# One transpose, three masks and four products moved between the first two units of a cached-attention block

## The chip, the cores and the metric

The kernel runs on one core of one Trainium2 chip. Its time is device microseconds of one execution; the median of three runs is compared. A profile of one further execution shows what each engine did and when: PE (matrix products), DVE (vector), ACT (scalar, also called ScalarE), POOL, and SP, the queue from which nearly all transfers are issued. The transfers themselves are carried out by the core's 16 DMA engines.

## The reference

One decode step of a transformer block with conditioning, for two batch rows of width 512. What matters here is the attention over a sliding block of the cache:

```
mod = silu(c) @ w_mod                      # six shifts, scales and gates
h = layernorm(x) * (1 + ca) + sa
q = h @ wq                                 # 32 query heads of 128, one position
k, v = last 4096 rows of the caches        # 8 key/value heads, each for 4 query heads
o = softmax(q k^T / sqrt(128)) v
x = x + ga * (o @ wo)
x = x + gb * (silu((layernorm(x) * (1 + cb) + sb) @ w1) @ w2)
```

All numbers are float32. 2 batch rows x 8 heads x 4096 rows x 128 numbers make 33.6 MB of keys and as much of values; with the weights the kernel reads 97.5 MB.

## The kernel before

All big tiles lie in `store`, three slots of 64 KB a partition, 8.39 MB each. A slot holds one load: first `w_mod` and `wq`, later one unit's keys or values, at the end the weights `wo`, `w1`, `w2`. The attention is cut into four units t = 0 to 3; a unit is one batch row and four key/value heads (`seq[t]`). Its keys `kt[t]` are one load of 8.39 MB, its values `vt[t]` another.

The loads of keys (k) and values (v) come in the order k0, k1, v0, k2, v1, k3, v2, v3 and take the slots 0, 1, 2 in turn. `fetch(n)` issues them up to the n-th. A load waits on SP until the last reader of its slot is done, and all later loads wait behind it, for SP runs its instructions in the order of the program. So k2 goes into slot 0 once the last product that reads unit 0's part of it is done, v1 into slot 1 after unit 1, and k3 into slot 2 after unit 0's values have been used.

The program is recorded operation by operation (class `Flow`; every operation therefore carries line 117 in the profile) and emitted in this order, with semaphore waits where an operation needs another engine's result or overwrites what another engine still reads. Each engine runs its own operations strictly in the order in which they were written down. For one unit they are:

- `scores(t)`: eight times DVE transposes an eighth of the keys in place (`STREAM_TRANSPOSE`, 128x2048) and PE multiplies it with the queries `qbd` (a group of four products; the profile shows two records for each). The eight groups fill the two halves f = 0, 1 of `bankA`, four each.
- the softmax, still inside `scores(t)`: maximum on DVE (`mx`), two small products on PE that spread it, `bias` and the exponentials on ACT, written into the first 1024 columns of the unit's key slot.
- `turn(t)`: DVE transposes these 1024 columns; four masks (`zp`, 128x512 each, a multiplication with a column of `key`) spread them over four copies, three on DVE and one on ACT; then four products with `gather` on PE collect them into `bankC`. They are the last readers of the slot.
- `spread(t)`: four ACT copies from `bankC` to `ptb`, the left operand of the products with the values.
- `values(t - 1, ...)`: the products of the unit before with its values, in two parts around `turn(t)`, and `collect(t - 1)`, which adds them up.

Unit 0 has no unit before it, so its `turn` and `spread` follow its softmax directly, and then `fetch(4)` issues k2.

Of the kernel before, what the change touches and what calls it, by code (L numbers as in the profile page):

```python
# [12 lines left out]
G = HQ // HKV  # L13
U = 4
# [121 lines left out]
def adaln_block(nc, x, k_cache, v_cache, wq, wo, w1, w2, c, w_mod, out):  # L136
# [7 lines left out]
    pe, dve, act, pool, sp = fl.pe, fl.dve, fl.act, fl.pool, fl.sp  # L144
# [4 lines left out]
    NK = W // 32  # L149
# [6 lines left out]
    bank_a = nc.alloc_psum_tensor("bankA", [P, 1024], F32).ap()  # L156
# [6 lines left out]
    def bank(tag):  # L163
        banks[tag].append(banks[tag].pop(0))
        return banks[tag][-1]
# [25 lines left out]
    def const(shape, name):  # L191
        return buf(name, *shape)
# [17 lines left out]
    kt, vt = {}, {}  # L210

    def load_cache(cache, t, where):
        hh, b = seq[t]
        sp.dma_start(
            where,
            cache[b, U * hh : U * hh + U, SK - W :, :].rearrange(
                "u (i n) d -> i u (n d)", n=NK
            ),
        )
        return where  # L220
# [59 lines left out]
    qbd = const([P, 2, 4, B, 4, 16], "qbd")  # L280
# [54 lines left out]
    for s0, s1, m in ((0, 2, m_a), (2, 6, m_b)):  # L335
        for k in range(4):
            v = wm[:, k].rearrange("p (s g m) -> p g s m", s=6, g=4)
            for g in range(4):
# [4 lines left out]
                    start=(k == 0),  # L343
                    stop=(k == 3),
# [22 lines left out]
    for n in range(2):  # L367
        for k in range(4):
            wv = wqt[:, k].rearrange("p (n s g m) -> p n g s m", n=2, s=4, g=G)
            for g in range(G):  # L370
# [4 lines left out]
                    start=(k == 0),  # L375
                    stop=(k == 3),
                )
    for n in range(2):
        qT = early(4, 4, 32)
        dve.transpose(qT.rearrange("p s j r -> p (s j r)"), q_ps[n])  # L380
        for g in range(G):
            r = slice(32 * g, 32 * g + 32)
# [8 lines left out]
        for i in range(4):  # L391
            r = slice(32 * i, 32 * i + 32)
# [7 lines left out]
    mx, bias = const([P, 1], "mx"), const([P, 1], "bias")  # L400
    o_all = bank("O")[:, : B * DH].rearrange("p (b d) -> p b d", b=B)

    def scores(t):
        hh, b = seq[t]
        kv = kt[t].rearrange("p (n j r) -> p n j r", n=NK, j=4)
        for f in range(2):
            for j in range(4):

                kT = kv[:, 64 * f : 64 * f + 64, j, :]
                dve.transpose(kT, kT)  # L410
                for u in range(U):
                    pe.matmul(
                        bank_a[32 * u : 32 * u + 16, 512 * f : 512 * f + 512],
                        qbd[:, hh, u, b, j, :],
                        kT[:, :, u:32:U],
                        start=(j == 0),
                        stop=(j == 3),
                    )
        mrow = kt[t][0:1, 3072:3200]
        pool.memset(mrow, 0.0)  # L420
        dve.tensor_reduce(mx, bank_a, axis=AX.X, op=ALU.max)
        mT = bank("B")
        pe.matmul(mT[0:1, :P], mx, sel, start=True, stop=True)
        dve.tensor_reduce(
            mg,
            mT[0:1, :64].rearrange("o (a g u) -> o g u a", g=G, u=U),
            axis=AX.X,
            op=ALU.max,
        )
        dve.tensor_copy(  # L430
            mrow.rearrange("o (u v a g) -> o u v a g", u=U, v=2, g=G)[:, :, 0],
            mg.rearrange("o g u -> o u g")[:, :, None, :].to_broadcast([1, U, 4, G]),
        )
        bp = bank("B")
        pe.matmul(bp[:, 0:1], mrow, negscale, start=True, stop=True)
        act.copy(bias, bp[:, 0:1])
        act.activation(
            kt[t][:, :1024], bank_a, AF.Exp, bias=bias, scale=SCALE, accum_out=rowsum[:, t : t + 1]
        )

    tp = bank("C")

    def turn(t):
        pr = kt[t][:, :1024]
        dve.transpose(pr, pr)
        xp = pr.rearrange("p (f k w) -> p f k w", f=2, w=32)
        zp = kt[t][:, 1024:3072].rearrange("p (n f k w) -> p n f k w", n=4, f=2, w=16)
        for n in range(4):
            if n < 3:
                dve.tensor_scalar(zp[:, n], xp[:, :, :, :16], key[:, n : n + 1], None, op0=ALU.mult)  # L450
            else:
                act.activation(zp[:, n], xp[:, :, :, :16], AF.Copy, scale=key[:, n : n + 1])
        for a in range(4):
            pe.matmul(
                tp[32 * a : 32 * a + 32],
                gather,
                zp.rearrange("p n f k w -> p (f k) n w")[:, :, :, G * a : G * a + G],
                start=True,
                stop=True,
            )  # L460

    def spread(t):
        for u in range(U):
            act.activation(
                ptb[:, :, G * u : G * u + G], tp.rearrange("p (n g) -> p n g", g=G), AF.Copy,
                scale=par[:, u : u + 1],
            )
# [3 lines left out]
    def values(t, n0, n1, n):  # L471

        for n0 in range(n0, n1, n):
            if n0 == 0:
                o_ps[t] = bank("D")
            c = n0 // n % (8 // n)
            r, d0 = 16 * n * c, n0 % 4 * DH
            pe.matmul(
                o_ps[t][r : r + 16 * n, d0 : d0 + n * DH],
                ptb[:, n0 : n0 + n, :].rearrange("p n w -> p (n w)"),  # L480
                vt[t][:, DH * n0 : DH * (n0 + n)],
                start=(n0 < 8),
                stop=(n0 + 8 >= NK),
                skip_group_check=True,
            )

    def collect(t):
        hh, b = seq[t]
        ob = vt[t][:, :512].rearrange("p (n d) -> p n d", n=4)
        act.copy(ob.rearrange("p n d -> p (n d)"), o_ps[t])  # L490
        for n in range(4):
            pe.matmul(
                o_all[64 * hh : 64 * hh + 64, b],
                pick[:, n].rearrange("p w i -> p (w i)"),
                ob[:, n],
                start=(n == 0),
                stop=(n == 3),
                skip_group_check=True,
            )
# [7 lines left out]
    def fetch(n):  # L507
        for i in range(fetched[0], min(n, len(order))):
            what, t = order[i]
            if what == "k":  # L510
                kt[t] = load_cache(k_cache, t, slot[i % 3])
            else:
                vt[t] = load_cache(v_cache, t, slot[i % 3])
        fetched[0] = max(fetched[0], n)
# [1 line left out]
    fetched = [0]  # L516
    fetch(3)
    for t in range(NP):
        scores(t)

        part = 64 if t > 1 else 32
        if t > 0:
            values(t - 1, 0, part, 4)
        turn(t)
        if t > 0:
            values(t - 1, part, NK, 2)
            collect(t - 1)
        spread(t)
        fetch(2 * t + 4)
    values(NP - 1, 0, 32, 4)  # L530
# [30 lines left out]
    for hh in range(HKV // U):  # L561
# [4 lines left out]
            start=True,  # L566
            stop=True,
# [141 lines left out]
```

## Time and profile before

| | us |
|---|---|
| median of 3 runs | 236.36 |
| the runs | 236.11 to 237.96 |
| the profiled execution, its own time | 234.84 |
| its span, first to last instruction | 233.4 |
| busy in it: PE / DVE / ACT / POOL | 157.7 / 108.9 / 30.7 / 7.3 |
| share of the DMA engines' time taken by SP's queue | 97.3% |

The profiled execution took 1.4 us more than its span, which is the time around the first and last instruction, and lies 1.5 us under the median of the runs. Lines of the profile give the start in us from the span's start, the length in us, then engine, line, operation, and what is written from what (without buffer numbers; the three slots are all `store`). "x8" counts instructions that were merged into a row. In brackets stands how long the engine was idle before, and what ended that. "us to landing" is the time from a transfer's issue until its last byte has arrived.

### The profile page before, as it was taken

Reading aid. Unit: us, or ns where it says so; the run is one execution under the profiler, and the core shown is the slowest. Engines: PE = TensorE matmul, PEld = TensorE weight load, DVE = VectorE, ACT = ScalarE, POOL = GpSimd, SP = SyncE. Lnnn points to the kernel's source line nnn. Section 1 sums busy time; section 2 is a strip of 40 time slices with the busy share of each in tenths; the row PEclk is TensorE's granted clock in tenths of the full one; section 3 lists DMA queues with packets and bytes.
Section 4 is the critical chain, followed back from the end, with each engine's and each line's share of the span. In section 5 each row is a group of like instructions: output and inputs, shape, how many; then the busy total and the mean of one; then the engine's idle time right before and its main releaser. Section 6 shows DMA issues by size and latency. Waiting matters only on the chain.

```text
span 233.4 us, 2509 instructions
## 1 busy us (share of the span) xinstructions
PE 157.7 (68%) x1114; PEld 43.9 (19%) x1114; DVE 108.9 (47%) x140; ACT 30.7 (13%) x54; POOL 7.3 (3%) x26
## 2 busy tenths in 40 slices
PE   0013905920699459977989869929987957989664
PEld 0002201310000000002610013410002332542232
DVE  6014130130999299965199924049965010020351
ACT  2003010010000232003050021050003050000501
POOL 4000000000000000000000000000000030000000
PEclk9999975875599859999999988988999997999999
DMA  7998998989989898998999999999999999989992
GB/s 270 439 540 371 404 494 359 531 359 461 438 371 528 371 507 374 404 494 382 441 416 404 494 407 449 404 404 486 416 438 438 416 404 421 455 376 461 404 410 99
DMA packets 2493, 97.67 MB, mean 419 GB/s; under 512 B 284, under 2 KB 308, under 8 KB 564
## 3 DMA queue, kind: packets, MB, share of 16 engines
q1 hardware_dynamic: 2460, 97.52, 97.3%
q8 instruction: 8, 0.13, 0.2%
q10 hardware_dynamic: 24, 0.01, 0.0%
q14 instruction: 1, 0.01, 0.0%
HBM read 97.53 MB, written 0.00 MB: 418 GB/s over the span
## 4 chain that ended last, share of the span: by engine, by line
DMA 47%; DVE 28%; PE 18%; another core or an unknown queue 3%; ACT 2%; issue 1%; SPq 0%; POOL 0%
DVE store L117 26%; DMA store<-in_B_w_dram 16%; DMA store<-in_A_wq_dram 15%; DMA store<-in_A_k_cache_dram 15%; PE bankD L117 11%; PE bankA L117 3%; DVE mx L117 2%; ACT store L117 2%; PE bankC L117 1%; PE bankB L117 1%; PE bankO L117 1%; SPq L117 0%; DVE qbd L117 0%; DVE mg L117 0%
## 5 line engine op out<-in xcount | busy, mean ns | idle before, releaser
L117 DVE STREAM_TRANSPOSE store<-store 128x2048 f32<-128x2048 f32 (+2 forms) x40 | 77.2, 1985 | 32.3 <-DMA store<-in_A_k_cache_dram 24.7
L117 PE MATMUL bankA<-store,qbd 128*16 128x512 f32 x256 | 64.7, 1086 | 18.6 <-DVE store L117 16.9
L117 PE MATMUL bankD<-store,ptb 128*32 128x256 f32 (+1 forms) x416 | 42.5, 445 | 3.1 <-DMA store<-in_A_v_cache_dram 3.1
L117 PE MATMUL bankD<-store 128*32 128x512 f32 x176 | 22.6, 666 | 10.6 <-DMA store<-in_A_wq_dram 8.3
L117 PEld LDWEIGHTS bankD<-store,ptb 128*32 128x32 f32 (+1 forms) x416 | 18.3, 120 | 25.1 <-issue 19.4
L117 PE MATMUL bankB<-store 128*32 128x256 f32 (+3 forms) x72 | 7.3, 473 | 21.8 <-DVE store L117 21.8
L117 PEld LDWEIGHTS bankA<-store,qbd 128*16 128x16 f32 x256 | 4.3, 96 | 73.7 <-DVE store L117 73.5
L117 ACT COPY bias<-bankB 128x1 f32<-128x1 f32 x4 | 0.6, 160 | 87.2 <-PE bankB L117 87.2
L117 PEld LDWEIGHTS bankD<-store 128*32 128x32 f32 x176 | 6.7, 123 | 25.8 <-issue 21.9
L117 ACT ACTIVATE ptb<-bankC,par 128x512 f32<-128x512 f32 x16 | 11.0, 689 | 3.1 <-PE bankC L117 2.7
L117 ACT COPY store<-bankD 128x512 f32<-128x512 f32 (+1 forms) x7 | 3.9, 559 | 49.3 <-PE bankD L117 49.3
L117 DVE TENSOR_REDUCE mx<-bankA 128x1 f32<-128x1024 f32 x4 | 4.9, 1225 | 8.7 <-PE bankA L117 8.7
L117 PEld LDWEIGHTS bankB<-store 128*32 128x32 f32 (+1 forms) x72 | 4.0, 150 | 24.4 <-DVE store L117 22.5
L117 PE MATMUL bankC<-store,gather 128*32 128x512 f32 x32 | 5.1, 717 | 4.8 <-DVE store L117 4.8
L117 POOL MEMSET store<- 128x128 f32 (+3 forms) x11 | 3.2, 294 | 139.1 <-PE bankA L117 115.9
L117 DVE RECIPROCAL store<-bankB 128x2 f32<-128x2 f32 x1 | 0.2, 170 | 15.8 <-PE bankB L117 15.8
L117 DVE STREAM_TRANSPOSE store<-bankD 128x512 f32<-128x512 f32 x2 | 1.4, 720 | 12.1 <-PE bankD L117 12.1
L117 DVE STREAM_TRANSPOSE store<-bankA 128x128 f32<-128x128 f32 (+1 forms) x2 | 0.7, 368 | 12.5 <-PE bankA L117 12.5
L117 PE MATMUL bankO<-store,pick 128*64 128x128 f32 x32 | 4.3, 279 | 2.9 <-ACT store L117 2.9
L117 ACT ACT_TABLE_LOAD x4 | 5.1, 1283 | 2.8 <-DVE id L117 2.8
L117 DVE BATCH_NORM_STATS2 store<-x_sp 128x6 f32<-128x128 f32 x1 | 0.3, 295 | 10.8 <-DMA x_sp<-in_A_x_dram 10.8
L117 DVE TENSOR_SCALAR store<-store,key 128x512 f32<-128x512 f32 x12 | 5.1, 483 | 0.1
(79 smaller groups left out, 60.5 us busy)
## 6 DMA issues: line engine op xcount, KB each, us to landing
store<-in_w_mod_dram SPq DMA_DIRECT2D x1, 6144.0 KB, 17.2
store<-in_A_wo_dram SPq DMA_DIRECT2D x1, 6144.0 KB, 22.7
store<-in_B_w_dram SPq DMA_DIRECT2D x1, 3584.0 KB, 30.9
store<-in_A_wo_dram SPq DMA_DIRECT2D x1, 2048.0 KB, 27.2
store<-in_B_w_dram SPq DMA_DIRECT2D x1, 2048.0 KB, 35.5
store<-in_B_w_dram SPq DMA_DIRECT2D x1, 1024.0 KB, 37.5
store<-in_B_w_dram SPq DMA_DIRECT2D x2, 256.0 KB, 37.7
store<-in_A_k_cache_dram SPq DMA_DIRECT2D x4, 32.9
```

Of the source, the lines that this page charges most:

```text
L117: ins = getattr(eng, method)(*args, **kw)
```

## The change

`scores` is taken apart into `keys` (the view of one eighth), `transposed` (its transpose) and `scores(t, i)` (its four products); the softmax becomes a function of its own, and so do the masks (`masked`) apart from the collecting products (`turn`). The computation stays the same. Three things then stand elsewhere, all at the seam of unit 0 and unit 1; units 2 and 3 are written in the same order as before.

```diff
+    def transposed(t, i):
+        dve.transpose(keys(t, i), keys(t, i))
...
-    def turn(t):
+    def masked(t):
         pr = kt[t][:, :1024]
         dve.transpose(pr, pr)
...
         for n in range(4):
-            if n < 3:
+            if 0 < t and n < 3:
                 dve.tensor_scalar(zp[:, n], xp[:, :, :, :16], key[:, n : n + 1], None, op0=ALU.mult)
             else:
                 act.activation(zp[:, n], xp[:, :, :, :16], AF.Copy, scale=key[:, n : n + 1])
+
+    def turn(t):
+        zp = kt[t][:, 1024:3072]
         for a in range(4):
             pe.matmul(
                 tp[32 * a : 32 * a + 32],
                 gather,
...
     for t in range(NP):
-        scores(t)
+        for i in range(8):
+
+            if (t, i) != (1, 0):
+                transposed(t, i)
+            scores(t, i)
+            if (t, i) == (1, 1):
+                turn(0)
+                spread(0)
+                fetch(4)
+        softmax(t)
+        if t == 0:
+            transposed(1, 0)
 
         part = 64 if t > 1 else 32
         if t > 0:
             values(t - 1, 0, part, 4)
+        masked(t)
+        if t == 0:
+            continue
         turn(t)
-        if t > 0:
-            values(t - 1, part, NK, 2)
-            collect(t - 1)
+        values(t - 1, part, NK, 2)
+        collect(t - 1)
         spread(t)
         fetch(2 * t + 4)
```

DVE, from the softmax of unit 0 to the maximum of unit 1. `128x64x32` is an eighth of the keys, `128x1024` the exponentials, `dma143` the semaphore of unit 1's keys:

```order
 L117 TENSOR_REDUCE mg<-bankB 1x16 [waits at_pe]
 L117 COPY store<-mg 1x4x16 [waits at_pool,at_dve]
+L117 STREAM_TRANSPOSE store<-store 128x64x32 [waits dma143]
 L117 STREAM_TRANSPOSE store<-store 128x1024 [waits at_act]
-L117 TENSOR_SCALAR store<-store,key 128x512 [waits at_dve]
-L117 TENSOR_SCALAR store<-store,key 128x512 x2
-L117 STREAM_TRANSPOSE store<-store 128x64x32 [waits dma143]
 L117 STREAM_TRANSPOSE store<-store 128x64x32 x7
 L117 TENSOR_REDUCE mx<-bankA 128x1 [waits at_pe]
```

The first of unit 1's eight transposes now stands ahead of the transpose that waits for ACT's exponentials, and the three masks are gone from between them and the other seven.

ACT at the same place, from the exponentials of unit 0 to its copies to `ptb`:

```order
 L117 ACTIVATE store,rowsum<-bankA,bias 128x1024 [waits at_act]
 L117 ACTIVATE store<-store,key 128x512 [waits at_dve]
+L117 ACTIVATE store<-store,key 128x512 x3
 L117 ACTIVATE ptb<-bankC,par 128x128x4 [waits at_pe]
 L117 ACTIVATE ptb<-bankC,par 128x128x4 [waits at_act] x3
```

All four masks of unit 0 now stand on ACT.

PE, from the two small products of unit 0's softmax to those of unit 1's. `bankA` rows are scores, four products a group, and the `bankC` row is the collecting products:

```order
 L117 MATMUL bankB<-sel,mx 1x128
 L117 MATMUL bankB<-negscale,store 128x1
+L117 MATMUL bankA<-store,qbd 16x512 x8
 L117 MATMUL bankC<-store,gather 32x512 x4
-L117 MATMUL bankA<-store,qbd 16x512 x32
+L117 MATMUL bankA<-store,qbd 16x512 x24
 L117 MATMUL bankB<-sel,mx 1x128
 L117 MATMUL bankB<-negscale,store 128x1
```

The collecting products moved behind two of unit 1's eight groups of scores. The issue of k2 on SP waits for them, as before; SP's own order is unchanged.

More of the change, by code (lines that the diff above doesn't have):

```diff
@@ L401, in adaln_block, with keys, scores, softmax @@
     o_all = bank("O")[:, : B * DH].rearrange("p (b d) -> p b d", b=B)
-    def scores(t):
-        hh, b = seq[t]
[L405 to L418, printed above, removed]
+    def keys(t, i):
+        f, j = divmod(i, 4)
+        v = kt[t].rearrange("p (n j r) -> p n j r", n=NK, j=4)
+        return v[:, 64 * f : 64 * f + 64, j, :]
+    def transposed(t, i):
+        dve.transpose(keys(t, i), keys(t, i))
+    def scores(t, i):
+        hh, b = seq[t]
+        f, j = divmod(i, 4)
+        for u in range(U):
+            pe.matmul(
+                bank_a[32 * u : 32 * u + 16, 512 * f : 512 * f + 512],
+                qbd[:, hh, u, b, j, :],
+                keys(t, i)[:, :, u:32:U],
+                start=(j == 0),
+                stop=(j == 3),
+            )
+    def softmax(t):
         mrow = kt[t][0:1, 3072:3200]
@@ L456, in turn @@
                 gather,
-                zp.rearrange("p n f k w -> p (f k) n w")[:, :, :, G * a : G * a + G],
+                zp.rearrange("p (n m w) -> p m n w", n=4, w=16)[:, :, :, G * a : G * a + G],
                 start=True,
```

## The prediction

> **What bounds the kernel now.** I read four views in this order: the page's slices (which resource is full all the time), the stages cut at the landings of the big loads (what a load costs), the sync queue's issues with their times to landing (how early each load is asked for), and the chain of waits (which names other things, so it has to be reconciled with the first three).
>
> Of the page's slices, the span in 40 parts, the DMA engines:
>
> ```profile
> DMA  7998998989989898998999999999999999989992
> ```
>
> Every slice stands at 8 or 9 tenths but the first, at 7, and the last, in which nothing is left to load. The stages, one cache load each (the second number is the length; the last two are the DMA engines' busy share and GB/s):
>
> ```profile
> core 0: us, PE busy (x) PEld busy (x) DVE busy (x) ACT busy (x) POOL busy (x), PEclk, DMA share, GB/s
> 57.80:77.10 19.30, 15.84 (x64) 1.08 (x64) 17.66 (x8) 0.00 (x0) 0.20 (x1) 0.86 1.00 435
> ...
> 96.67:116.04 19.37, 16.33 (x140) 5.41 (x140) 9.31 (x10) 2.09 (x4) 0.00 (x0) 1.00 1.01 433
> ...
> 174.30:193.65 19.35, 13.74 (x120) 5.67 (x116) 5.17 (x8) 5.33 (x9) 2.08 (x5) 0.98 1.01 434
> ...
> 2.00:228.00 226.00, 155.28 (x1054) 42.49 (x1058) 107.55 (x135) 30.14 (x53) 6.62 (x20) 0.91 0.99 428
> ```
>
> PE, DVE and ScalarE all have idle time in these stages, the DMA engines none. Each 8.39 MB load takes 19.3 to 19.4 us at 433 to 435 GB/s, whether ScalarE works 0 or 5.33 us in it and DVE 5 or 18. Over 2 to 228 us the share is 0.99. Even a queue without one gap would gain only 226 x (1 - 428/434) = 3.1 us in the whole kernel. Now the issues on the sync queue (start, length), and behind them the times from issue to landing, one answer for each issue in the same order:
>
> ```profile
> 51.00 0.60 SPq L117 DMA_DIRECT2D store<-in_A_v_cache_dram  x1
> 86.38 0.54 SPq L117 DMA_DIRECT2D store<-in_A_k_cache_dram  x1
> 111.87 0.54 SPq L117 DMA_DIRECT2D store<-in_A_v_cache_dram  x1
> 118.81 0.54 SPq L117 DMA_DIRECT2D store<-in_A_k_cache_dram  x1
> ```
>
> ```profile
> store<-in_A_v_cache_dram SPq DMA_DIRECT2D x1, 45.7
> store<-in_A_k_cache_dram SPq DMA_DIRECT2D x1, 29.7
> store<-in_A_v_cache_dram SPq DMA_DIRECT2D x1, 23.7
> store<-in_A_k_cache_dram SPq DMA_DIRECT2D x1, 36.1
> ```
>
> Added up, the values of unit 0 land at 96.7, the keys of unit 2 at 116.1, the values of unit 1 at 135.6, the keys of unit 3 at 154.9: 19.4, 19.5 and 19.3 apart. The issues are 35.4, 25.5 and 6.9 apart. Landings therefore do not follow issues: each load waits in a first-come queue behind the one before it. An issue counts only if it comes after the queue has run empty. The spare time is the landing of the load before, less the issue: 10.3 us for the keys of unit 2, 4.2 for the values of unit 1, 16.8 for the keys of unit 3. What comes off it is the start of a transfer on an empty queue, which the kernel's first load shows:
>
> ```profile
> 0.74 0.39 SPq L117 DMA_DIRECT2D store<-in_w_mod_dram  x1
> 0.74:1.74 1.00, 0.00 (x0) 0.00 (x0) 0.55 (x3) 0.00 (x0) 0.49 (x2) 1.00 0.00 0
> 1.76:2.00 0.24, 0.00 (x0) 0.00 (x0) 0.21 (x2) 0.00 (x0) 0.00 (x0) 1.00 7.62 2253
> ```
>
> No byte moves for 1.0 us after the issue, then all engines do (a packet is booked whole where it starts, hence the 7.62 in so short a stretch). So 9.3, 3.2 and 15.8 us remain.
>
> The chain of waits (start, length) tells it otherwise:
>
> ```profile
> 118.81 36.12 DMA store<-in_A_k_cache_dram
> ...
> 191.58 37.51 DMA store<-in_B_w_dram
> 229.08 0.04 issue
> 229.13 1.78 PE bankA L117 x56
> ```
>
> It follows a DMA back to its issue and from there to DVE and PE. But a load of 19.4 us that needs 36.12 has queued for the other 16.7; the step back should go to the load ahead of it. What sets the end is the queue: filled from 1.76 us, last landings around 229 to 230, then about 4 us of products and DVE work up to 233.4.
>
> **The change part by part.** All of it lies between the softmax of unit 0 and the second unit's scores. The rows there (start, length):
>
> ```profile
> 81.69 1.25 DVE L117 STREAM_TRANSPOSE store<-store 128x1024 f32<-128x1024 f32 x1 [1.90 <-ACT store L117]
> 82.97 0.72 ACT L117 ACTIVATE store<-store,key 128x512 f32<-128x512 f32 x1 [1.31 <-DVE store L117]
> 82.97 1.28 DVE L117 TENSOR_SCALAR store<-store,key 128x512 f32<-128x512 f32 x3
> 84.16 17.66 DVE L117 STREAM_TRANSPOSE store<-store 128x2048 f32<-128x2048 f32 x8
> ...
> 84.39 1.94 PE L117 MATMUL bankC<-store,gather 128*32 128x512 f32 x8 [4.17 <-DVE store L117]
> ...
> 88.71 1.98 PE L117 MATMUL bankA<-store,qbd 128*16 128x512 f32 x8 [0.16 <-DVE store L117]
> ...
> 104.00 1.23 DVE L117 TENSOR_REDUCE mx<-bankA 128x1 f32<-128x1024 f32 x1 [2.18 <-PE bankA L117]
> ...
> 110.75 1.07 PE L117 MATMUL bankC<-store,gather 128*32 128x512 f32 x8 [0.59 <-DVE store L117]
> ...
> 116.06 17.66 DVE L117 STREAM_TRANSPOSE store<-store 128x2048 f32<-128x2048 f32 x8 [5.45 <-DMA store<-in_A_k_cache_dram]
> ```
>
> *First transpose of unit 1 on DVE.* One of eight in 17.66 us is 2.21 us. Its keys landed one load ahead of unit 0's values, at about 77, so nothing holds it and it runs from 79.8 to 82.0, in place of the 1.90 us that DVE idled ahead of 81.69, behind the exponentials. It overhangs by 82.0 - 81.7 = 0.3: the transpose of the probabilities moves to 82.0 to 83.3.
>
> *Masks.* DVE sheds 1.28 us; ScalarE gets four passes of 0.72 = 2.9 us instead of one, 83.3 to 86.2, while PE works on scores. DVE goes straight on with seven transposes, 7 x 2.21 = 15.5, to 98.8; before it ended at 84.16 + 17.66 = 101.8. Unit 1's scores end 3.0 us earlier.
>
> *Collecting products behind two groups of scores.* On PE group (1,0) runs 82.1 to 84.1 (2.0 each, from the 1.98 row), group (1,1) from the end of its transpose, 85.5, to 87.6; the masks are done at 86.2. The four products follow at 87.6. They took 1.94 in this place and 1.07 in unit 1's, so they end between 88.7 and 89.6, where before it was 86.3. Group (1,2) could start at 87.8 and is held 0.9 to 1.8 us; a group needs 0.2 less than a transpose (1.98 against 2.21), so the backlog of five groups shrinks by 1.1, and at worst 0.7 us is left at the last. The maximum of unit 1 (104.00) comes at 101.0 to 101.7.
>
> *Spread and fetch.* The four copies to ptb start at 88.7 to 89.6 and are needed by unit 0's values after 103: covered. On the sync queue the keys of unit 2 are issued 2.3 to 3.3 us later, at 88.7 to 89.7. The number and order of the DMAs stay; nothing is queued behind this one until the values of unit 1. The spare falls from 9.3 to 6.0 to 7.0 us: cost 0, covered by the unit 0 values that are still moving until 96.7. POOL clears a row for unit 1 once PE has read that piece of the slot, in the middle of its groups; what needs it comes after unit 1's maximum: 0.
>
> *What follows.* Values of unit 1 are issued 2.3 to 3.0 us earlier, 108.8 to 109.6, keys of unit 3 at 115.8 to 116.5. Both wait that much longer in the queue: gain 0. DVE ends unit 1 earlier and waits for the keys of unit 2 8 us instead of 5.45; they land at 116.1 as before, and from there both kernels run alike. Should a later issue cost more than the rows show, the bound is the 3.3 us by which it moves; should an earlier one gain, the 3.0.
>
> Sum: 233.4 + 0 + the 1.4 outside the span = 234.84, the profiled execution's own time. The median of the three runs is 1.5 above that, 236.36, and they reach from 236.11 to 237.96. I forecast the median: 236.4 us.
>
> Here two rules of the Trainium skill pull apart. Its page "Perfetto Trace Analysis", under "Optimization Strategies" for DMA, says that where the matmul engine idles, the engines that block the critical path are to be sped up; by that the change should pay about 3 us. Under "Identifying the Most-Contended Engine" the same page says to work first on what is fullest, by transferred bytes in the case of DMA; by that the change pays nothing. The stages' 433 to 435 GB/s in every row bear out the second.
>
> **The rivals.**
>
> *Faster by the chain.* If the chain were right that the issue of unit 3's keys sets the time, 118.81 moving to 115.8 would shorten everything behind it by 3.0 us: 233.3 us, 1.3% faster. (The rule of the Trainium skill's page "Perfetto Trace Analysis", "Optimization Strategies", comes to the same time.) For it speaks only the chain; against it that landings are 19.4 apart whatever the issues. Chance 0.03.
>
> *A small gain that the profile does not show.* The values of unit 1 have the least spare, 3.2 us. If the timed runs' extra 1.5 us came from a gap there, the earlier issue would win it back: 234.9, still within 1%. Against it: the stage 96.67 to 116.04 has share 1.01, and a gap would need compute over 3 us later than in the profile. Chance 0.05.
>
> *Slower: the queue runs dry before unit 2's keys.* Those now hang on a ScalarE row of masks and on PE's strict order behind two groups. If that issue came after 96.7 - 1.0 = 95.7, each us more would be a us lost; over 1% slower needs an issue at about 98.1, 8.4 us after my latest estimate, and gives 238.8 or more. For it speaks that this is the one load issued later; against it 6 us of spare, and that nothing in the place lasts longer than 2.9 us. Chance 0.02.
>
> *The change does not do what it says.* PE's backlog, or ScalarE's 2.9 us, could eat the 3.0 us, so that unit 1 ends where it did. The values of unit 1 then keep their 3.2 us of spare: 236.4 as well. Chance 0.06, with the same result as the forecast.
>
> **How the numbers follow.** The forecast itself, issues moved and landings not, has 0.82; the case without effect on unit 1 0.06; the small gain 0.05; together 0.93 within 1%, about what a measurement of this kernel can tell from no change, as its three runs spread over 0.8%. Faster: 0.03 for the chain and 0.01 for what I don't see, 0.04. Slower: 0.02 for the dry queue and 0.01, 0.03. The range is set by the runs, not by the change: from the profiled execution's 234.8, which is also the small gain's end, to the highest run, 238.0. It leaves out the chain's 233.3 and the dry queue's 238.8, together under 1 in 10, and as much again for a median that falls outside for other reasons.
>
> **What would show it.** Right: the eighth-part transposes of unit 1 as 1 and 7 around the 1024-wide one; four ScalarE masks in a row; the unit 2 keys issued at 88.7 to 89.7 and taking about 27 us to land, the unit 1 values issued near 109 and taking 26 to 27; DVE waiting about 8 us for the keys of unit 2 and starting them at 116.1; DMA shares of 1.00 in the same stages. Wrong: a stage with a share clearly under 1 between 86 and 120, a landing of unit 2's keys away from 116, or a span more than 2 us from 233.4.

## The result, and the profile after

| | before | after |
|---|---|---|
| median of 22 runs, us | 237.35 | 235.13 |
| the runs, us | 234.83 to 239.25 | 234.44 to 237.35 |
| ratio, 95% interval | | 0.9937 (0.9912 to 0.9963) |
| profiled execution: its time / span, us | 234.84 / 233.4 | 234.89 / 233.6 |

The changed kernel is 0.6% faster, some 1.5 us. That is within 1%, but clear of noise, and no change was forecast. The two profiles do not show it: they are 0.05 us apart. With 22 runs the kernel before stands at 237.35 instead of the 236.36 of the first three, so its profiled execution was one of its quickest, 2.5 us under the median; the one after is 0.2 us under. (Ratios and counts of spans leave out disturbed runs, over 1.5% above the quickest; the profile of the delayed kernel e3 is of such a run, and only its times up to 157 us are used.)

Every place that the change touches went as forecast. Rows of the profile after, in order of time, from DVE, ACT, PE and the sync queue (start, length):

```profile
79.97 18.77 DVE L117 STREAM_TRANSPOSE store<-store 128x2048 f32<-128x2048 f32 x9
...
83.42 2.56 ACT L117 ACTIVATE store<-store,key 128x512 f32<-128x512 f32 x4 [1.51 <-DVE store L117]
...
87.45 1.10 PE L117 MATMUL bankC<-store,gather 128*32 128x512 f32 x8
...
88.63 0.54 SPq L117 DMA_DIRECT2D store<-in_A_k_cache_dram  x1
...
100.92 1.23 DVE L117 TENSOR_REDUCE mx<-bankA 128x1 f32<-128x1024 f32 x1 [2.19 <-PE bankA L117]
...
108.78 0.54 SPq L117 DMA_DIRECT2D store<-in_A_v_cache_dram  x1
...
116.17 17.66 DVE L117 STREAM_TRANSPOSE store<-store 128x2048 f32<-128x2048 f32 x8 [8.65 <-DMA store<-in_A_k_cache_dram]
```

DVE's first row is unit 1's first transpose, the one of the exponentials, and the other seven in one piece; the masks follow one another on ACT; the keys of unit 2 are issued at 88.63 (before 86.38), the maximum of unit 1 comes at 100.92 (104.00), the values of unit 1 are issued at 108.78 (111.87), and DVE waits 8.65 us for the keys of unit 2 instead of 5.45. The times to landing of the three issues that moved, keys of unit 2, values of unit 1, keys of unit 3:

```profile
store<-in_A_k_cache_dram SPq DMA_DIRECT2D x1, 27.5
...
store<-in_A_v_cache_dram SPq DMA_DIRECT2D x1, 26.7
...
store<-in_A_k_cache_dram SPq DMA_DIRECT2D x1, 39.2
```

88.63 + 27.5, 108.78 + 26.7 and 115.72 + 39.2 give 116.1, 135.5 and 154.9, the same landings as before to 0.1 us. In this pair of executions all three shifts ended in the queue. The gain must therefore lie in executions of the kernel before that its profile does not show. The spans bear this out: of the 95 executions of the kernel before whose span is on record, 59 are over 234.5 us, of the changed kernel's 22 only 4.

### The profile page after: what moved, and what is told of

The parts are those of the page before. It is cut to its first block, busy times and chain, and to the rows that moved or that the text cites. A ratio compares the mean times of both kernels' runs of the same rounds, so it can differ in the third digit from the quotient of the medians.

```text
span 233.6 us, 2509 instructions
## 1 busy us (share of the span) xinstructions
PE 156.7 (67%) x1114; PEld 44.9 (19%) x1114; DVE 107.5 (46%) x137; ACT 32.6 (14%) x57; POOL 7.3 (3%) x26
## 4 chain that ended last, share of the span: by engine, by line
DMA 47%; DVE 27%; PE 19%; another core or an unknown queue 4%; ACT 1%; issue 1%; SPq 0%; POOL 0%
DVE store L117 25%; DMA store<-in_A_k_cache_dram 17%; DMA store<-in_A_wq_dram 15%; DMA store<-in_B_w_dram 14%; PE bankD L117 12%; PE bankA L117 3%; DVE mx L117 2%; PE bankC L117 1%; ACT store L117 1%; PE bankO L117 1%; PE bankB L117 1%; DVE qbd L117 0%; SPq L117 0%; DVE mg L117 0%
## 5 line engine op out<-in xcount | busy, mean ns | idle before, releaser
L117 PE MATMUL bankD<-store,ptb 128*32 128x256 f32 (+1 forms) x416 | 41.2, 438 | 1.7 <-ACT ptb L117 1.7
L117 PE MATMUL bankD<-store 128*32 128x512 f32 x176 | 23.7, 668 | 9.7 <-DMA store<-in_A_wq_dram 7.3
L117 PE MATMUL bankC<-qbd,store 128*128 128x512 f32 (+1 forms) x10 | 6.2, 744 | 0.0
L117 ACT ACTIVATE store<-store,key 128x512 f32<-128x512 f32 x7 | 4.7, 716 | 5.5 <-DVE store L117 5.5
L117 DVE COPY store<-sbT 128x8 f32<-128x8 f32 x1 | 1.0, 1008 | 9.4 <-POOL store L117 9.4
```

Source lines behind the costliest of these rows:

```text
L117: ins = getattr(eng, method)(*args, **kw)
```

## The experiments

Two theories. *Late issue*: in most executions of the kernel before, the values of unit 1 are issued so late that the queue has run dry, and the three microseconds by which the change brings them forward win that back. *Tail*: the queue is never dry, and the difference lies behind the last landings, or comes with something else that moved. Of each run the decisive number is how far units 2 and 3 start their first transposes apart, for these starts are the landings of the loads in front of and behind the values of unit 1: two loads without a gap make 2 x 19.36 = 38.7 us. In the profile of the kernel before it is 38.9; its second start, behind the 116.06 of the first:

```profile
154.96 2.31 DVE L117 STREAM_TRANSPOSE store<-store 128x2048 f32<-128x2048 f32 x1 [12.46 <-DMA store<-in_A_k_cache_dram]
```

**e1: the kernel before again.** No edit.

> The kernel before, unchanged, for the spread of its own executions and a second profile. The timed runs of the kernel before had a median 2.5 us above the lowest, those of the changed kernel 0.7, while both profiles show a queue without a gap. Theory 'late issue': in most executions, not in the profiled one, the values of unit 1 are issued after the queue has run dry, because PE is at half clock after unit 1's softmax and the eight products of unit 0's values, which stand ahead of the collecting products, take up to 7 us instead of 3.65. Then the ratio is 1.000 (0.997 to 1.003), the spans spread over 3 us or more, and a profile of a slow one shows the values of unit 1 issued after 114.5 us and landing after 136. Theory 'tail': the time is lost behind the last landings, by the phase of the clock; then a slow one shows all landings at the same times as before and a longer stretch behind them.

Ratio 0.998 (0.994 to 1.002). In the profile the values of unit 1 are issued at 111.80, units 2 and 3 start at 115.81 and 155.59, 39.8 apart: 1.1 us lost, with the issue no later than in the first profile (111.87):

```profile
111.80 0.54 SPq L117 DMA_DIRECT2D store<-in_A_v_cache_dram  x1
...
115.81 17.66 DVE L117 STREAM_TRANSPOSE store<-store 128x2048 f32<-128x2048 f32 x8 [5.27 <-DMA store<-in_A_k_cache_dram]
155.59 2.31 DVE L117 STREAM_TRANSPOSE store<-store 128x2048 f32<-128x2048 f32 x1 [13.40 <-DMA store<-in_A_k_cache_dram]
```

So the kernel before stands right at an edge there. The expected issue after 114.5 was not needed; how 1.1 us could be lost at 111.80 stands in the section on the prediction.

**e2: collecting products first.** The kernel before; unit 0's values no longer stand ahead of unit 1's collecting products.

```diff
-        if t > 0:
+        if t > 1:
             values(t - 1, 0, part, 4)
         turn(t)
+        if t == 1:
+            values(t - 1, 0, part, 4)
```

> The kernel before, with the first eight products of unit 0's values moved behind unit 1's collecting products; nothing of the change. Late issue: the values of unit 1 are issued near 111 us whatever the clock, so most of the gain comes back, ratio 0.993 to 0.997, with spans closer together. Tail: the queue does not care, ratio 1.000 (0.997 to 1.003).

Ratio 1.005 (1.002 to 1.009), slower, which neither theory had expected. In its profile the stage ahead of these products (the last three numbers are PE's granted clock, DMA share, GB/s), and the products:

```profile
107.00:111.00 4.00, 0.32 (x4) 0.23 (x8) 2.52 (x4) 1.67 (x3) 0.00 (x0) 0.62 0.72 311
```

```profile
110.69 1.94 PE L117 MATMUL bankC<-store,gather 128*32 128x512 f32 x8 [4.17 <-DVE store L117]
```

With nothing in front of the collecting products PE idled 4.17 us, and they ran at half clock and took 1.94 us instead of 1.07. The values of unit 1 were issued at 112.67 instead of earlier, and units 2 and 3 started at 115.88 and 156.50, 40.6 apart. The means failed, but the result has the sign that a later issue should have.

**e3: the change, with unit 1 held back on DVE.**

```diff
+            if (t, i) == (1, 7):
+                for _ in range(2):
+                    dve.transpose(keys(t, i)[:, :44], keys(t, i)[:, :44])
```

> The changed kernel, with two thirds of unit 1's last eighth transposed twice more ahead of its transpose (two and a half more transposes undo each other), some 3.1 us on DVE, so that unit 1 ends when it did before while the keys of unit 2 stay issued late. Late issue: the gain is gone, ratio 1.000 (0.997 to 1.003), values of unit 1 issued near 112. Tail, or a gain from the later issue of unit 2's keys: ratio stays 0.992 to 0.996.

Two such transposes undo each other. Issue at 112.12, starts at 116.27 and 155.90, 39.6 apart. Ratio 0.997 (0.993 to 1.0005): the profile speaks for the late issue, the ratio excludes neither.

**e4: only the transpose moved.** The change without the masks on ACT and without the later place of the collecting products.

```diff
-            if 0 < t and n < 3:
+            if n < 3:
...
-            if (t, i) == (1, 1):
-                turn(0)
-                spread(0)
-                fetch(4)
...
         masked(t)
-        if t == 0:
-            continue
         turn(t)
...
```

> Only the first transpose of unit 1 moved into unit 0's softmax; masks and collecting products as before. DVE then ends unit 1 by 1.9 us earlier instead of 3.0. Late issue: the values of unit 1 are issued near 110.0 and part of the gain comes, ratio 0.994 to 0.998. Tail: 1.000 (0.997 to 1.003).

Ratio 0.994 (0.991 to 0.998): the whole gain as far as it can be told, with unit 2's keys issued at 86.39 as before. So it does not come from their later issue. Values of unit 1 issued at 109.64, units 2 and 3 started at 115.88 and 154.73, 38.9 apart.

**e5, e11, e12: only the issue moved.** The changed kernel with one extra product that reads unit 1's slot, so that the transfer that overwrites it waits; its result is not used. It stands behind m of the 48 products that follow the collecting ones: m = 30 in e5 (shown), 0 in e11 (the control, 32 in place of 92), 44 in e12 (120).

```diff
         turn(t)
-        values(t - 1, part, NK, 2)
+        if t == 1:
+            values(t - 1, part, 92, 2)
+            pe.matmul(bank("B")[0:1, :P], kt[t][:, 1024:1025], sel, start=True, stop=True)
+            values(t - 1, 92, NK, 2)
+        else:
+            values(t - 1, part, NK, 2)
```

> The changed kernel with one small extra product that reads unit 1's slot again after 30 of unit 0's 48 remaining products, so that the issue of the values of unit 1 moves from 108.8 back to about 112 us and nothing else moves. Late issue: the gain is gone, ratio 1.000 (0.997 to 1.004), and the last landing of these values is 0.5 to 1.5 us further than 19.4 us behind the one before. If the gain came from unit 1 ending earlier or from the later issue of unit 2's keys: ratio stays 0.991 to 0.997.

> Control for the run with the late issue: the same small extra product in the changed kernel, but directly behind unit 1's collecting products, so that the values of unit 1 are issued near 109 us. Late issue: the gain is there as in the changed kernel, ratio 0.991 to 0.997, units 2 and 3 start their transposes 38.7 us apart. If the extra product itself had cost the gain: 0.997 to 1.004.

> The same extra product after 44 of the 48, so that the values of unit 1 are issued near 113.5 to 114.5 us. Late issue: worse than before, ratio 1.003 to 1.010, units 2 and 3 start 40.8 to 42.5 us apart. Any other cause: as in the control.

Ratios: e11 0.9935 (0.991 to 0.996), e5 1.001 (0.998 to 1.005), e12 1.003 (1.000 to 1.007). The extra product costs nothing where it stands early; where it holds the issue back, the gain is gone. That e12 is slower than the kernel before is not clear of noise, but e11 and e12, timed together, do not overlap: e11's highest run is 236.33 us, e12's lowest 236.75. The extra product overshot in e5: the issue came at 113.06, not near 112, which is later than in three of the four profiles of the kernel before. So e5 does not restore the kernel before exactly, but its 12 spans, 233.3 to 236.7 us, spread like the 233.1 to 236.5 there. And the keys of unit 3 were still issued early in both, at 116.59 and 115.71, so their earlier issue is not where the gain came from. The sync queue's issue and DVE's waits for the keys of units 2 and 3, first in e11, then in e12:

```profile
108.73 0.54 SPq L117 DMA_DIRECT2D store<-in_A_v_cache_dram  x1
...
115.89 17.66 DVE L117 STREAM_TRANSPOSE store<-store 128x2048 f32<-128x2048 f32 x8 [8.57 <-DMA store<-in_A_k_cache_dram]
154.69 4.50 DVE L117 STREAM_TRANSPOSE store<-store 128x2048 f32<-128x2048 f32 x2 [12.43 <-DMA store<-in_A_k_cache_dram]
```

```profile
113.47 0.54 SPq L117 DMA_DIRECT2D store<-in_A_v_cache_dram  x1
...
116.25 17.66 DVE L117 STREAM_TRANSPOSE store<-store 128x2048 f32<-128x2048 f32 x8 [8.94 <-DMA store<-in_A_k_cache_dram]
156.81 2.31 DVE L117 STREAM_TRANSPOSE store<-store 128x2048 f32<-128x2048 f32 x1 [14.16 <-DMA store<-in_A_k_cache_dram]
```

38.8 apart in the one, 40.6 in the other (a little less than the 40.8 expected); in e5 40.9, which is 2.2 us lost where 0.5 to 1.5 were expected. DVE works at the same times up to unit 2 in both; what follows the late issue is late, and nothing else.

**e6: the other half of the change.** Masks and collecting products moved, the transpose not (it stands with the other seven again).

> The change without its first part: masks on the scalar engine and collecting products behind two groups of scores, but the first transpose of unit 1 where it was. DVE ends unit 1 by 1.2 us earlier, so the values of unit 1 are issued near 110.6. Late issue: this is still ahead of the point near 111.8, so 0.994 to 0.998. If only the transpose in the idle time of DVE pays: 1.000 (0.997 to 1.003).

Ratio 0.997 (0.993 to 1.0004). The values of unit 1 were issued at 111.68, not at 110.6. PE ahead of that:

```profile
106.00:110.00 4.00, 4.00 (x12) 1.12 (x10) 2.52 (x4) 1.50 (x3) 0.00 (x0) 0.57 1.13 492
```

```profile
105.28 5.35 PE L117 MATMUL bankD<-store,ptb 128*64 128x512 f32 x16
110.56 1.06 PE L117 MATMUL bankC<-store,gather 128*32 128x512 f32 x8
```

The clock was 0.57 here, and the eight products of unit 0's values took 5.35 us instead of 3.65, so the collecting products came behind them. Units 2 and 3 started 38.7 apart all the same: with unit 1 more than 1 us earlier, the half clock still left the issue ahead of the edge. The middle of the ratio's interval fits the half gain that was expected; it does not exclude none.

**e7: PE kept busy in unit 1's softmax.** The kernel before with one product of 1.1 us, result not used, ahead of the one that spreads the maximum.

> The kernel before, with one extra product of 1 us on PE in unit 1's softmax, where PE waits for the maximum; its result is not used. Late issue made worse by the half clock: PE stays busy, the clock is halved less often between 104 and 111 us, ratio 0.994 to 0.999 and fewer spans over 236. If the clock there does not matter: 1.000 (0.997 to 1.003), or slower by up to 0.3 us where the extra product delays the maximum's.

Ratio 1.000 (0.996 to 1.003). Values issued at 112.10, units 2 and 3 39.2 apart. The product ended after the maximum was there and pushed the issue 0.2 us back, so this run tells nothing of the clock.

**e8: fewer values ahead in units 2 and 3.** The changed kernel with `part = 32` in all units.

> The changed kernel, in which units 2 and 3 too put eight products instead of sixteen ahead of their collecting products, so that the values of unit 2 and the first part of the output weights are issued about 3 us earlier. If late issues there cost some executions of the changed kernel their 1 to 2 us: ratio 0.988 to 0.992, spans closer to 233.3. If not: as the changed kernel, 0.991 to 0.997.

Ratio 0.995 (0.992 to 0.998), as the changed kernel and no better. The values of unit 2 went out at 145.00 instead of 146.65, the first of `wo` at 183.56 instead of 187.10. These issues have enough spare, and the changed kernel's remaining spread has another cause. Part of it lies where the second theory looked, behind the last landings: the last packets of the weights ended at 229.8 us in the profile after, 229.6 in e4 and 229.7 in e8, nothing was lost at the seam, and the spans are 233.6, 234.3 and 234.8. PE's granted clock from 220 to 225 us was 0.79, 0.68 and 0.52 in them, which fits; no run tried it.

**e9, e10: two more profiles of the kernel before.**

> The kernel before, unchanged, for a profile of an ordinary execution: the two so far had spans of 233.4 and 233.9, while half of the others lie above 234.8. Late issue: if the span is over 234.8, PE shows a half clock somewhere between 104 and 111 us, the values of unit 1 are issued at 112.5 or later, and land 20.5 us or more behind the keys of unit 2. Tail: these land 19.4 behind, and the extra time lies after the last weights' landing.

> The same once more, with the same expectations, since one execution can be one of the quick ones.

e10 was a quick one: span 233.5, values issued at 111.93, starts 39.0 apart. e9 had a span of 235.1. Its rows: two stages with PE's clock (third number from the end), PE's values and collecting products, the issue:

```profile
104.00:107.00 3.00, 1.11 (x10) 0.48 (x8) 1.64 (x3) 0.00 (x0) 0.00 (x0) 1.00 1.41 612
107.00:111.00 4.00, 4.00 (x12) 1.21 (x14) 2.52 (x4) 2.09 (x4) 0.00 (x0) 0.57 0.76 328
```

```profile
106.89 5.35 PE L117 MATMUL bankD<-store,ptb 128*64 128x512 f32 x16
112.18 1.06 PE L117 MATMUL bankC<-store,gather 128*32 128x512 f32 x8
...
113.30 0.53 SPq L117 DMA_DIRECT2D store<-in_A_v_cache_dram  x1
```

The clock was 0.57 from 107 to 111, about 3.4 us at half, where it had been 1.00 in the first profile; the eight products of unit 0's values took 5.35 us instead of 3.65 (106.51 to 110.16 then), so the collecting products behind them waited for PE and not for the masks, and the issue came at 113.30 instead of 111.87. Units 2 and 3 started at 116.11 and 156.47, 40.4 apart:

```profile
116.11 17.66 DVE L117 STREAM_TRANSPOSE store<-store 128x2048 f32<-128x2048 f32 x8 [5.11 <-DMA store<-in_A_k_cache_dram]
156.47 2.31 DVE L117 STREAM_TRANSPOSE store<-store 128x2048 f32<-128x2048 f32 x1 [13.76 <-DMA store<-in_A_k_cache_dram]
```

That is 1.6 us lost, 1.5 more than in the first profile, and the span is 1.7 longer than there. The values landed at 113.30 + 23.8 = 137.1, 21.0 behind the keys of unit 2. The expectation of the late issue is met in each number.

All profiles by the time of issue, one execution each:

| | issue of unit 1's values, us | starts of units 2 and 3 apart, us |
|---|---|---|
| e8, e11, after, e4 | 108.60, 108.73, 108.78, 109.64 | 38.6, 38.8, 38.7, 38.9 |
| e6 | 111.68 | 38.7 |
| e1 | 111.80 | 39.8 |
| before | 111.87 | 38.9 |
| e10 | 111.93 | 39.0 |
| e7, e3 | 112.10, 112.12 | 39.2, 39.6 |
| e2 | 112.67 | 40.6 |
| e5 | 113.06 | 40.9 |
| e9, e12 | 113.30, 113.47 | 40.4, 40.6 |

Up to 111.7 the distance is 38.6 to 38.9, whatever else was changed; from 111.8 to 112.1 it is 38.9 to 39.8, and from 112.7 on about 2 us are lost. Four different means brought the issue there: the clock, PE's order, DVE, and an extra reader.

## Why the prediction was wrong

The step that failed is the spare of unit 1's values, put at 4.2 us less 1.0, that is 3.2. It is a size: the rival "a small gain that the profile does not show" named this place and its price, and was given 0.05 because the spare seemed too large. It was mis-sized at both ends. The queue in short stages around the seam (the last two numbers are the share of packets that start in it, and GB/s), in the kernel before, in e9 with its issue at 113.30, and in the kernel after:

```profile
113.00:113.60 0.60, 0.60 (x19) 0.42 (x15) 0.00 (x0) 0.00 (x0) 0.00 (x0) 1.00 0.25 109
113.60:114.00 0.40, 0.40 (x13) 0.28 (x9) 0.00 (x0) 0.00 (x0) 0.00 (x0) 1.00 3.49 1311
114.00:114.50 0.50, 0.50 (x16) 0.38 (x12) 0.00 (x0) 0.00 (x0) 0.00 (x0) 1.00 0.91 393
```

```profile
113.60:114.00 0.40, 0.40 (x16) 0.23 (x12) 0.00 (x0) 0.00 (x0) 0.00 (x0) 1.00 0.01 0
114.00:114.50 0.50, 0.50 (x16) 0.31 (x12) 0.00 (x0) 0.00 (x0) 0.00 (x0) 1.00 0.00 0
114.50:115.00 0.50, 0.50 (x16) 0.26 (x8) 0.00 (x0) 0.00 (x0) 0.00 (x0) 1.00 4.39 1442
```

```profile
113.60:114.00 0.40, 0.31 (x8) 0.00 (x0) 0.00 (x0) 0.03 (x1) 0.00 (x0) 1.00 2.06 860
114.00:114.50 0.50, 0.00 (x0) 0.00 (x0) 0.00 (x0) 0.50 (x2) 0.00 (x0) 1.00 2.12 918
```

First, the load ahead needs its successor not when it lands, at 116.1, but when the first of the 16 DMA engines has done its part. In the packet records of the traces each load closes with 16 packets of 4 bytes, read here as one for each engine, and those of the keys of unit 2 begin at 113.63 in the kernel before and have all come by 115.6; 13 have come by 114.3. In e9 no data packet starts between 113.6 and 114.5. Second, the start of a transfer was read from its first packets alone. The new load's start in e9 at 114.63, 1.33 us after the issue, but the last engine gets its first at 116.39, 3.1 us after it; in e5 and e12 that is 1.3 to 3.4 and 1.3 to 4.0 us. So the spare was 113.6 - 111.87 - 1.3 = 0.4 us for the first engine, not 3.2, and none for an engine that is done early and served late. The table puts the edge at 111.7 to 111.8, so the first profile, at 111.87, had none left.

This answers e1 too. There one engine, idle since 114.8 at the latest, got its first packet at 115.04, 3.2 us after the issue, and that packet took 3.92 us instead of 2.42. Seven more of 2.42 end at 135.9, where this load's last packet ends; the other 15 engines are done by 134.9, and in the first profile all 16 by 135.1. The landing is that of the last engine, and this one engine is the 0.9 us that e1 lost more than the first profile.

Point by point:

- *The queue bounds the kernel, an issue counts only if the queue has run dry*: right, with dry to be read engine by engine. It fits the seam in all fourteen profiles, and explains why the chain of waits, with its 3.0 us, was wrong. Of the two rules of the Trainium skill's page "Perfetto Trace Analysis" the second holds, as long as the queue has something to carry.
- *Each load takes 19.3 to 19.4 us at 433 to 435 GB/s*: not all. Two of the seven cache loads took 19.5 us at 430 GB/s, and one of them is that of unit 1's values:

```profile
116.04:135.58 19.54, 17.72 (x92) 2.26 (x83) 17.66 (x8) 3.24 (x5) 0.20 (x1) 1.00 1.00 430
```

  The 0.2 us over 19.36 are too little to tell by themselves, but they stand at the place that was dismissed.
- *The shifts at the seam*: the issues and the maximum right to 0.2 us; the masks took 2.56 us where 2.9 was worked out, and DVE waited 8.65 instead of 8.
- *Values of unit 1 earlier: gain 0*: wrong. 3.1 us earlier takes them from the edge to a spare of about 3.6 for the first engine and 1 for one served 4 us late, and that is what pays: moved back, the gain goes (e5, e12), and with the same extra product early it stays (e11).
- *Keys of unit 2 later: cost 0*: right. Worked out in the new way, their spare is smaller than stated, 96.7 - 2.4 - 1.3 - 88.63 = 4.4 us for the first engine and 1.7 for one served 4 us late, but it is there, and the landing of 116.1 stayed.
- *Masks and collecting products*: they were costed together with the transpose. e4 shows that the transpose alone brings the issue to 109.64 and the gain with it; what the others add cannot be told from nothing.
- *One profile stands for the runs*: wrong, and the range alone was made from the runs. I took the 1.5 us between the profiled execution and the median for spread, although it was the one hint of executions unlike the profile.

How the executions of the kernel before come to differ is shown in part. In e9 it was PE's clock, and e6 shows the same clock without a loss where unit 1 is earlier. Over its 95 executions the spans have a median of 235.35 us where the mean granted clock is under 0.90, and 234.3 where it is not. In the changed kernel it is 234.5 and 233.6, so a lower clock goes with a longer span there too, where the seam has spare. The Trainium skill's page "TensorE: Matmul & The Clock Gate", Part 1, says that the clock is gated in free-running windows of 3.4 us that do not start with the kernel. That fits the traces: the half clock lasts about 3.4 us in e9 and in e6, and stands at other places in each execution, between 107 and 111 in e9 and nowhere near in the first profile. e1 lost 1.1 us without it, by one engine served late; which share each has in the executions without a profile was not tried.

## What to carry to other kernels

Where transfers bound a kernel, work out for each load by how much its issue comes ahead of the moment at which the first DMA engine is done with the load in front, not of its landing, and take off what an issue needs to reach the engines: here the moment lay 2.4 us ahead of the landing, and an issue needed 1.3 us to the first engine and 3 to 4 to the last. Issues 4.6 us or more ahead of the start on the keys of unit 2 lost nothing, those 4.2 to 4.0 ahead lost 0.2 to 1.1 us, those 3.2 ahead or less about 2. Such a place, with under 1 us of spare in the profile, cost 1.5 us in other executions here, and a profile quicker than the median of its runs is a reason to look for one. Where PE's products stand ahead of such an issue, count them at half clock as well: here 5.35 us instead of 3.65.

## What the runs showed of the hardware

A gap in the queue was not made up: in e9 the loss at the values of unit 1 stays to the end of the span. After an issue onto a dry queue the first packets started 1.0 us later at the kernel's begin and 1.3 us later in e5, e9 and e12, and the last of the 16 engines started 3.1 to 4.0 us after the issue in these three. The Trainium skill's page "DMA: Bandwidth & Descriptors", Specifications, gives about 0.6 us to the first byte on this path; the measured values, from the start of the issue to the first packet, are about twice that. The loss does not follow the issue alone: from 111.87 to 113.30 (e9) 1.4 us of issue cost 1.5 us, but e1 lost 0.9 us more than the first profile with an issue 0.07 us earlier, and e12, issued 0.4 us after e5, lost no more than it.

Taking work away from in front of a waiting PE group made it slower (e2): after 4.17 us of idleness it ran at half clock, and 1.07 us of products became 1.94. That the idleness is the cause is not shown: in e6 and e9 the half clock came while PE was busy.
